# Third quarter of w1 ahead of batch 0's last q slot, tile 1's turn ahead of the second quarter's matmuls, new planned load rates, and one masked product for batch 0's kv

## The chip, the cores and the metric

The kernel runs on one core of a Trainium2 chip. The metric is the device time of the whole program in microseconds (us). Engines are named as in the profile: PE (matmul), PEld (its weight loads), DVE (VectorE), ACT (ScalarE), POOL (GpSimd), SP (SyncE).

## The reference

```python
def _attn_ref(q, k, v, g_norm):                     # 8 batches, 8 heads, 576 rows, 64 wide
    kv = np.einsum('bhsd,bhse->bhde', k, v)
    out = np.einsum('bhsd,bhde->bhse', q, kv)
    rms = np.sqrt(np.mean(out * out, axis=-1, keepdims=True) + 1e-06)
    return out / rms * g_norm

def _moe_ref(x, g_ln, w_ch1, w_ch2):                # x: the above as (8, 576, 512)
    xn = (x - mu) / np.sqrt(var + 1e-06) * g_ln
    return x + np.maximum(xn @ w_ch1, 0.0) @ w_ch2  # 512 -> 2048 -> 512
```

## The kernel before

The kernel does not fix the order of its instructions by hand. Each piece of work is added as a step with an engine, a planned duration, a key (lower goes first) and its inputs; a small planner then plays the program through, with planned rates for the loads, and the start times of that play give each engine its order. Once built, the order is fixed: an engine waits for the next instruction in its order even if a later one is ready (in the changed kernel PE stood 0.66 us for one load while the next one in its order had landed, see below). A planned rate moves no byte, but can change the order.

The rows are handled in 36 tiles of 128. A tile of attention output is normed (DVE and ACT), turned, that is transposed, by PE (`xT` in the profiles), multiplied with the four quarters of w1 (16 matmuls a group in the first two blocks of four tiles) and then with the four quarters of w2. A q slot is the part of a batch's q that one tile needs. The loads of the first 44 us run through one queue from POOL (the comments on the right and the lines with dots are added, for what is left out):

```python
    pool_load(("k", 0, 0), load_kv(kb, k, 0, 0, 4), rate6)
    # ... k, v and q of batch 0, in pieces
    pool_load(("q", 0, 1), load_slot(qp[0], q, 0, 1), rate1)
    load_w(0, 1)                                              # first quarter of w1
    pool_load(("q", 0, 2), load_slot(qp[0], q, 0, 2), rate1)
    load_w(1, 1)
    pool_load(("q", 0, 3), load_slot(qp[0], q, 0, 3), rate1)  # last q slot: tile 3 needs it
    load_w(2, 1)
    load_w(3, 1)
    # ... later: w2's first quarter, k and v of batch 1, w2's second quarter, q of batch 1,
    #     the other quarters of w2
```

The product kv of two heads is a 128x128 block of which only the two 64x64 blocks on the diagonal are wanted. Before, ACT zeroed the target once, and then DVE and ACT each copied one of the blocks out of PSUM, one after the other:

```python
        for u in (0, 1):
            eng, cost = (("DVE", dve_cost), ("ACT", act_cost))[u]
            ab.append(add(eng, *cost(64 * (h1 - h0) // 2), -59 + i, [s, z0],
                          lambda h0=h0, h1=h1, u=u: kv_out(
                              0, h0 // 2, h1 // 2, (nc.vector, nc.scalar)[u], u == 1)))
```

In the planner, PE may hold still for a step that is ready up to `NEAR` = 0.35 us later, if its key is below -3:

```python
                    near = [d for d in cand if d[0] <= t + NEAR and d[1] < c[1] - 0.7
                            and c[0] + c[2].occ > d[0] + 0.1 and (e != "PE" or d[1] < -3)]
```

Of the kernel before, what the change touches and what calls it, by code (L numbers as in the profile page):

```python
# [14 lines left out]
def kernel(  # L15
# [11 lines left out]
    nc = tc.nc  # L27
    f32 = mybir.dt.float32
# [68 lines left out]
    def add(eng, occ, dur, key, deps, fn, dma=None, alloc=None, main=False, lag=0.0):  # L97
        s = Step()
        s.eng, s.occ, s.dur, s.key, s.fn = eng, occ, dur, key, fn
        s.deps = [d for d in deps if d is not None]  # L100
        s.dma, s.alloc, s.main, s.frees, s.behind = dma, alloc, main, None, None
        s.start = s.done = None
        s.lag = lag
        steps.append(s)
        return s
# [83 lines left out]
    def dve_cost(n, rate=0.96, fix=0.075):  # L189
        return n / 1000 / rate + fix, n / 1000 / rate + fix + 0.085  # L190
# [14 lines left out]
    nc.vector.memset(eps_attn, EPS_ATTN)  # L205
    eps_ln = consts.tile([128, 1], f32, name="eps_ln")
    nc.vector.memset(eps_ln, EPS_LN)
    warm = consts.tile([128, 1], f32, name="warm")
    nc.scalar.activation(warm, eps_ln, func=AF.Sqrt)

# [49 lines left out]
    def load_slot(dst, src, b, t, h0=0, h1=H):  # L260
        def fn():
            nc.gpsimd.dma_start(  # L262
                dst[:, t, h0:h1, :],
                src[b, h0:h1, 0:512, :].rearrange("h (p t) d -> p t h d", t=4)[:, t, :, :])
        return fn, 128 * (h1 - h0) * 256
# [65 lines left out]
    def pool_load(name, fnb, rate=425.0, deps=()):  # L331
        fn, nb = fnb
        s = add_dma("POOL", 0, deps, fn, nb, rate)
        load.setdefault(name, []).append(s)
# [4 lines left out]
    def load_w(c, which):  # L339
        dst, src = ((w1, w1_src), (w2, w2_src))[which - 1]  # L340
        def fn():
            if which == 1:
                nc.gpsimd.dma_start(dst[c], src[:, :, c * 512:(c + 1) * 512])  # L343
            else:
                nc.gpsimd.dma_start(dst[c], src[:, c * 4:(c + 1) * 4, :])
        pool_load(("w", which, c), (fn, 512 * 512 * 4))

    def identity_fn():
        make_identity(nc, identity)
# [1 line left out]
    def load_w_kv1():  # L351
# [17 lines left out]
    load_w(0, 1)  # L369
    pool_load(("q", 0, 2), load_slot(qp[0], q, 0, 2), rate1)  # L370
    load_w(1, 1)
    pool_load(("q", 0, 3), load_slot(qp[0], q, 0, 3), rate1)
    load_w(2, 1)
    load_w(3, 1)


    z0 = add("ACT", 0.5, 0.6, -90, [],
             lambda: nc.scalar.memzero(kv_pack[0].rearrange("p a b -> p (a b)")))
    z1 = [pool_do(0.5, f) for f in (
        lambda: nc.gpsimd.memset(qp[0][no_fifth(0), 4, :, :], 0.0),  # L380
        lambda: nc.gpsimd.memset(qp[1][no_fifth(1), 4, :, :], 0.0),
# [78 lines left out]
    def kv_out(b, h0, h1, eng, upper):  # L460
        dst, src = kv_pack[b % 3], att[b]["kv", h0]
        p = slice(D, 128) if upper else slice(0, D)
        f = slice(D, 128) if upper else slice(0, D)
        if eng is nc.scalar:
            eng.copy(dst[p, h0:h1, f], src[p, h0:h1, f])
        else:
            eng.tensor_copy(dst[p, h0:h1, f], src[p, h0:h1, f])  # L467

    def t_out(n, h0=0, h1=H):
        bs, t = TILES[n]  # L470
# [190 lines left out]
    for h0, h1 in PARTS:  # L661
        add_q_turn_pe(0, 0, load["q", 0, 0, h0], -57 + h0 / 4, ("DVE", "ACT")[h0 // 4], h0, h1)
    for t in (1, 2, 3):
        q_turned = add_q_turn_pe(0, t, load["q", 0, t], (-4.5, pos[1] - 3.7, pos[3] - 9)[t - 1],
                                 ("ACT", "ACT", "DVE")[t - 1])
        if t == 2:
            behind_first = q_turned
# [3 lines left out]
    for i, (h0, h1) in enumerate(((0, 4), (4, 6), (6, 8))):  # L671
        hps = range(h0 // 2, h1 // 2)
        w = (h1 - h0) / 8
        s = add("PE", 1.36 * w, 1.36 * w + 0.25, -60 + i, load["v", 0, h0] + [k0p[h0 // 4]],
                lambda hps=hps, i=i: kv_mm(0, hps), alloc="kvt")
        ab = [s]
        for u in (0, 1):
            eng, cost = (("DVE", dve_cost), ("ACT", act_cost))[u]
            ab.append(add(eng, *cost(64 * (h1 - h0) // 2), -59 + i, [s, z0],
                          lambda h0=h0, h1=h1, u=u: kv_out(  # L680
                              0, h0 // 2, h1 // 2, (nc.vector, nc.scalar)[u], u == 1)))
        s.frees = ab[-1]
        kvs.append(ab[1:])
        if i == 0:
            kv_first = s
        else:
            urgent.append(s)
        kv_mm_done = s
# [104 lines left out]
    def plan_tile(n):  # L793
        bs, t = TILES[n]
        m, i = divmod(n, 4)
        p = pos[n]
        dn = done[n]
        deps = []
        for b in bs:
            deps += adone[b]["kv"] + adone[b]["qT", t]  # L800
        if n >= 12:
            deps.append(main_at(okey[n] - EARLY))
        def cost(c, h0, h1):
            return c((h1 - h0) * D)
        halves = PARTS if n in HALVED else ((0, H),)

        q0 = okey[n] if n // 4 not in FINE else p - 12
        xs = []
        for h0, h1 in halves:
            hh = dict(h0=h0, h1=h1)  # L810
            w = (h1 - h0) / H
            q0 = p - 12 if n // 4 in FINE else okey[n]
            d = kvs[len(xs)] + [adone[0]["qT", 0][len(xs)]] if n in HALVED else deps
            o = add("PE", 0.23 * len(bs) * w, 0.23 * len(bs) * w + 0.2, okey[n], d,
                    lambda hh=hh: t_out(n, **hh), alloc="out")
            if n in HALVED:
                urgent.append(o)
            sq = add("ACT", *cost(act_cost, h0, h1), q0 + 4,
                     [o] + [done[n - 3]["red"] if n >= 3 else None], lambda hh=hh: t_sq(n, **hh))
            red = add("DVE", 0.6 * w, 0.6 * w + 0.08, q0 + 5, [sq], lambda hh=hh: t_red(n, **hh))  # L820
            o.frees = xg = add("DVE", *cost(dve_cost, h0, h1), q0 + 5.5, [sq, gn_done],
                               lambda hh=hh: t_xg(n, **hh))
            rms = add("ACT", 0.2, 0.3, q0 + 5.8, [red], lambda hh=hh: t_rms(n, **hh))
            inv = add("DVE", 0.12, 0.2, q0 + 6.5, [rms], lambda hh=hh: t_inv(n, **hh))
            xdeps = [inv, xg]
            if n >= XB:
                xdeps.append(done[n - XB]["store"])
            extra = 0.08 if n < N_SUM else 0
            occ, dur = cost(dve_cost, h0, h1)
            xs.append(add("DVE", occ + extra, dur + extra, q0 + 7, xdeps, lambda hh=hh: t_x(n, **hh)))  # L830
        for b in bs:
            adone[b].setdefault("outs", []).append(o)
        dn["red"] = red
        few = n < N_SUM
        mean = add("DVE", 0.15 if few else 0.8, 0.2 if few else 0.9, q0 + 7.5, xs, lambda: t_mean(n))
        m1_before = blk[m - 3]["m1done"] if m >= 3 else None
        turned = []
        for h0, h1 in ((0, 4), (4, 8)) if n in HALF_TURN else halves:
            ff = dict(f0=h0 * D, f1=h1 * D)
            w = (h1 - h0) / H  # L840
            xc = add("DVE", 0.6 * w + 0.06, 0.6 * w + 0.15, q0 + 8, [mean, load["gl"][0]],
                     lambda ff=ff: t_xc(n, **ff))
            if n < N_PE_TURN:
                tp = add("PE", 0.23 * w, 0.23 * w + 0.22, q0 + 8.2, [xc, ident, m1_before],
                         lambda ff=ff: t_turn_pe(n, **ff), alloc="kvt")
                if n in HALVED:
                    urgent.append(tp)
                tp.frees = add("ACT", *cost(act_cost, h0, h1), q0 + 8.5, [tp],
                               lambda ff=ff: t_turn_out(n, **ff))
                turned.append(tp.frees)  # L850
            else:
                turned.append(add_dma("SP", q0 + 9, [xc, m1_before], lambda: t_turn_dma(n),
                              0.5e3, 1.0, occ=1.235, lat=0.25, tail=0.42))
        dn["xT"] = turned
        if n in HALVED:
            behind_first.deps.append(tp)
        var = [mean]
        if few:
            var.append(add("ACT", 0.68, 0.83, p + 5, xs + dn["xT"], lambda: t_s2(n)))
        blk[m].setdefault("var", []).extend(var)  # L860
        if m in FINE or i == 3:
            vd = var if m in FINE else blk[m]["var"]
            e = last_pos[n if m in FINE else 4 * m] - 6
            if few:
                vd = [add("DVE", 0.33, 0.4, e, vd, lambda: b_var(n))]
            s = add("ACT", 0.2, 0.3, e + 1, vd, lambda: b_std(n))
            r = add("DVE", 0.12, 0.2, e + 2, [s], lambda: b_rstd(n))
            for j in ((n,) if m in FINE else range(4 * m, 4 * m + 4)):
                done[j]["rstd"] = r
# [139 lines left out]
```

## Time and profile before

| what | before |
|---|---|
| time, median of 3 runs | 294.01 us (293.96 to 294.26) |
| PE busy | 283.5 us, 97% of a span of 292.3 |
| ACT, DVE, POOL busy | 49%, 56%, 22% |
| second quarter of w1 lands (PE waits for it) | 19.09 us |
| q of batch 1 lands (ACT permutes it, PE turns it) | 38.82 us |

PE is the bound, so the question is where PE stands still. The first line of part 4 of the page, "by engine", sums up the chain of work that ended last:

```profile
PE 85%; DMA 10%; POOL 3%; issue 0%; ACT 0%; DVE 0%; POOLq 0%
```

The 10% of DMA are the two loads of the table. For exact sums I use **holes**: the start of a matmul less the start of the one before it and its pitch, 0.0557 us for 128 columns and 0.2158 for 512, both read from the trace's start times. The profile's own idle figure is some 0.16 us smaller for the same hole, since the end of a matmul is modelled. In the kernel before, the holes from 17 us on are 1.42 (w1's second quarter), 0.29 and 0.23 (behind tile 1's turn) and 0.55 (turn of batch 1's q). There are none above 0.06 after that.

### The profile page before, as it was taken

How to read it: one execution, taken by the hardware profiler on the slowest of the kernel's cores; microseconds unless marked ns; L12 is line 12 of the kernel's file. 1: busy time of each engine (PE TensorE's matmuls, PEld its weight loads, DVE VectorE, ACT ScalarE, POOL GpSimd, SP SyncE). 2: the span in 40 equal slices, each digit the busy share in tenths (PEclk: the TensorE clock that was granted, in tenths of full speed). 3: DMA queues.
4: the chain of work that ended last, by engine and by line, in shares of the span. 5: the costliest groups of instructions: out<-in, count | busy, mean ns of one | idle time of the engine just before them, and what ended most of it. 6: DMA issues, size and time to landing. Idle time of an engine off the chain costs nothing.

```text
span 292.3 us, 5180 instructions
## 1 busy us (share of the span) xinstructions
PE 283.5 (97%) x2056; PEld 160.9 (55%) x2056; DVE 164.3 (56%) x358; ACT 143.2 (49%) x292; POOL 65.7 (22%) x93
## 2 busy tenths in 40 slices
PE   8769999999999999999999999999999999999995
PEld 6659944977745445444544445444544444444444
DVE  1587038569973997557655775477557755320022
ACT  3469953787846612761276127611761177017400
POOL 8983230106407204504060406000000000000000
PEclk9999999999999999999999999999999999999999
DMA  7999999944999998996999499912201310220012
GB/s 97 184 199 205 204 198 171 251 85 66 177 201 112 162 138 206 117 167 161 134 119 219 60 184 116 195 54 91 56 18 54 92 54 18 57 87 21 0 74 72
DMA packets 108716, 35.60 MB, mean 122 GB/s; under 512 B 87187, under 2 KB 104467, under 8 KB 108692
## 3 DMA queue, kind: packets, MB, share of 16 engines
q0 software_dynamic: 72624, 18.35, 66.6%
q1 hardware_dynamic: 35828, 16.79, 25.9%
q8 instruction: 16, 0.26, 0.4%
q10 hardware_dynamic: 240, 0.13, 0.2%
q14 instruction: 8, 0.07, 0.1%
HBM read 36.70 MB, written 9.44 MB: 158 GB/s over the span
## 4 chain that ended last, share of the span: by engine, by line
PE 85%; DMA 10%; POOL 3%; issue 0%; ACT 0%; DVE 0%; POOLq 0%
PE mm_ps L640 41%; PE mm_ps L621 33%; DMA qb<-in_q_dram 7%; PE mm_ps L606 5%; DMA w<-in_moe_w_ch_dram 3%; PE out_ps L475 3%; PE kv_ps L452 2%; POOL qp L262 1%; POOL vb L241 1%; PE xT_ps L556 1%; POOL kb L241 1%; PE qT_ps L411 0%; POOL w L343 0%; ACT qp L391 0%; POOL identity masks.py:197 0%
## 5 line engine op out<-in xcount | busy, mean ns | idle before, releaser
L640 PE MATMUL mm_ps<-w,m 128*128 128x512 bf16 (+2 forms) x608 | 129.8, 368 | 0.0
L621 PE MATMUL mm_ps<-xT,w 128*128 128x512 bf16 x448 | 100.6, 379 | 0.0
L628 ACT ACTIVATE m<-mm_ps 128x512 bf16<-128x512 f32 x112 | 66.8, 597 | 51.2 <-PE mm_ps L621 50.3
L640 PEld LDWEIGHTS <-m 128*128 128x128 bf16 x608 | 57.1, 98 | 60.3
L621 PEld LDWEIGHTS <-w 128*128 128x128 bf16 x448 | 43.1, 98 | 48.8
L497 DVE TENSOR_REDUCE ss<-sq 128x8 f32<-128x512 f32 (+1 forms) x37 | 24.6, 668 | 47.7 <-ACT sq L488 47.7
L647 DVE SCALAR_TENSOR_TENSOR x<-mm_ps,rstd,x 128x512 f32<-128x512 f32 (+2 forms) x38 | 27.2, 719 | 42.1 <-PE mm_ps L640 42.1
L488 ACT ACTIVATE sq<-out_ps 128x512 f32<-128x512 f32 (+1 forms) x37 | 21.5, 583 | 38.9 <-PE out_ps L475 38.9
L606 PE MATMUL mm_ps<-xT,w 128*128 128x128 bf16 x512 | 30.9, 219 | 1.6 <-DMA w<-in_moe_w_ch_dram 1.3
L606 PEld LDWEIGHTS <-w 128*128 128x128 bf16 x512 | 29.3, 98 | 2.8 <-DMA w<-in_moe_w_ch_dram 1.4
L549 DVE SCALAR_TENSOR_TENSOR xc<-x,mv,gl 128x512 bf16<-128x512 f32 (+1 forms) x38 | 27.2, 722 | 1.1
L492 DVE TENSOR_TENSOR xg<-out_ps,gn 128x512 f32<-128x512 f32 (+1 forms) x37 | 24.7, 668 | 0.2
L613 ACT ACTIVATE m<-mm_ps 128x512 bf16<-128x512 f32 x32 | 18.7, 598 | 3.3 <-PE mm_ps L606 2.9
L730 POOL COPY mark<-xT 128x1 bf16<-128x1 bf16 x15 | 7.0, 464 | 58.0 <-DMA xT<-xc 54.0
L501 ACT ACTIVATE rms<-ss,eps_attn 128x8 f32<-128x8 f32 (+1 forms) x37 | 11.0, 298 | 12.4 <-DVE ss L497 12.2
L527 DVE TENSOR_TENSOR x<-xg,inv 128x512 f32<-128x512 f32 x24 | 16.6, 691 | 0.8
L543 DVE BATCH_NORM_STATS2 stats<-x 128x6 f32<-128x512 f32 x24 | 16.6, 690 | 0.5
L475 PEld LDWEIGHTS <-qT 128*128 128x128 bf16 x160 | 11.4, 98 | 7.2 <-ACT qT L391 1.1
L475 PE MATMUL out_ps<-kv_pack,qT 128*128 128x128 bf16 x160 | 14.5, 219 | 0.7 <-ACT qT L391 0.7
L467 DVE CAST kv_pack<-kv_ps 64x256 bf16<-64x256 f32 (+2 forms) x17 | 6.6, 390 | 9.8 <-PE kv_ps L452 5.9
L452 PEld LDWEIGHTS <-kp 128*128 128x128 bf16 (+1 forms) x168 | 10.3, 99 | 2.5 <-DVE kp L393 0.4
L269 POOL DMA_DIRECT2D qp<-in_q_dram x5 | 11.4, 2282 | 0.7 <-issue 0.7
(63 smaller groups left out, 176.9 us busy)
## 6 DMA issues: line engine op xcount, KB each, us to landing
out_dram<-x SPq DMA_DIRECT2D x30, 256.0 KB, 2.9
w<-in_moe_w_ch_dram POOLq DMA_DIRECT2D x8, 512.0 KB, 12.2
vb<-in_v_dram POOLq DMA_DIRECT2D x6, 512.0 KB, 11.9
kp<-in_k_dram POOLq DMA_DIRECT2D x5, 512.0 KB, 9.3
qp<-in_q_dram POOLq DMA_DIRECT2D x5, 512.0 KB, 10.8
out_dram<-x SPq DMA_DIRECT2D x10, 128.0 KB, 3.4
qb<-in_q_dram POOLq DMA_DIRECT2D x2, 512.0 KB, 18.2
qp<-in_q_dram POOLq DMA_DIRECT2D x10, 64.0 KB, 9.3
```

What stands on the lines that cost most here:

```text
L475: nc.tensor.matmul(o3[:, hp, :], lhsT=att[b]["qT"][:, 4 * t + hp, :], rhs=kv_pack[b % 3][:, hp, :], start=(i == 0), stop=(i == len(bs) - 1))
L488: nc.scalar.activation(sq[:, h0:h1, :], st[n]["ps", h0][:, h0:h1, :], func=AF.Square)
L492: nc.vector.tensor_mul(xg[:, h0:h1, :], st[n]["ps", h0][:, h0:h1, :], gn.to_broadcast([128, h1 - h0, D]))
L497: nc.vector.tensor_reduce(ss[:, h0:h1, :], st[n]["sq"][:, h0:h1, :], axis=AX.X, op=ALU.add)
L527: nc.vector.tensor_mul(x, st[n]["xg"], inv)
L549: nc.vector.scalar_tensor_tensor(xc[:, f0:f1], in0=st[n]["x"][:, f0:f1], scalar=blk[m]["mv"][:, i, 0:1], in1=gl[:, f0:f1], op0=ALU.subtrac ...
L606: nc.tensor.matmul(ps[:, d, :], lhsT=w1[c][:, kk, d * 128:(d + 1) * 128], rhs=blk[m]["xT"][:, kk, i * 128:(i + 1) * 128], start=(kk == 0), ...
L613: nc.scalar.activation(st[n]["m1"][:, c, :, :], st[n]["m1ps", c], func=AF.Relu)
L621: nc.tensor.matmul(ps, lhsT=w1[c][:, kk, d * 128:(d + 1) * 128], rhs=blk[m]["xT"][:, kk, :], start=(kk == 0), stop=(kk == nKm - 1))
L628: nc.scalar.activation(blk[m]["m1", c][:, d, :], blk[m]["m1ps", g], func=AF.Relu)
L640: nc.tensor.matmul(st[n]["m2ps", f0], lhsT=m1_piece(n, c, d), rhs=w2[c][:, d, f0:f1], start=(c == 0 and d == 0), stop=(c == 3 and d == 3))
L647: nc.vector.scalar_tensor_tensor(x[:, f0:f1], in0=st[n]["m2ps", f0], scalar=blk[m]["rstd"][:, i, :], in1=x[:, f0:f1], op0=ALU.mult, op1=AL ...
```

## The change

Its intent: have w1's third quarter in time for a PE that gets ahead; fill PE's wait for w1's second quarter with the turn of tile 1; shorten the path from kv to tile 0 by taking the copies off ACT. The planned rates of the first two quarters are set closer to what the loads take.

```diff
+    diag = consts.tile([128, 1, 128], f32, name="diag")
+    nc.vector.memset(diag, 0.0)
+    for p in (slice(0, D), slice(D, 128)):
+        nc.vector.memset(diag[p, :, p], 1.0)
@@ planned rate of a weight load
-        pool_load(("w", which, c), (fn, 512 * 512 * 4))
+        pool_load(("w", which, c), (fn, 512 * 512 * 4), 355.0 if which == 1 and c < 2 else 425.0)
@@ order of loads
+    load_w(2, 1)
     pool_load(("q", 0, 3), load_slot(qp[0], q, 0, 3), rate1)
-    load_w(2, 1)
     load_w(3, 1)
-    z0 = add("ACT", 0.5, 0.6, -90, [],
-             lambda: nc.scalar.memzero(kv_pack[0].rearrange("p a b -> p (a b)")))
@@ kv of batch 0: the pair of copies (above) gives way to
+        nc.vector.tensor_mul(kv_pack[b % 3][:, h0:h1, :], att[b]["kv", h0][:, h0:h1, :],
+                             diag.to_broadcast([128, h1 - h0, 128]))
@@ key of the turn of q slots 1 to 3
-(-4.5, pos[1] - 3.7, pos[3] - 9)[t - 1]
+(-4.5, pos[1] - 3.7, -3.2)[t - 1]
@@ key of tile 0's first half x
-q0 + 7
+q0 + (4.8 if h1 < H else 7)
@@ key of a tile's turn
-q0 + 8.2
+-3.5 if n == 1 else q0 + 8.2
```

More of the change, by code (lines that the diff above doesn't have):

```diff
@@ L462, in kv_out, with kv_out_masked @@
         p = slice(D, 128) if upper else slice(0, D)
-        f = slice(D, 128) if upper else slice(0, D)
-        if eng is nc.scalar:
-            eng.copy(dst[p, h0:h1, f], src[p, h0:h1, f])
-        else:
-            eng.tensor_copy(dst[p, h0:h1, f], src[p, h0:h1, f])
+        eng.tensor_copy(dst[p, h0:h1, p], src[p, h0:h1, p])
+    def kv_out_masked(b, h0, h1):
+        nc.vector.tensor_mul(kv_pack[b % 3][:, h0:h1, :], att[b]["kv", h0][:, h0:h1, :],
+                             diag.to_broadcast([128, h1 - h0, 128]))
     def t_out(n, h0=0, h1=H):
@@ L663 @@
     for t in (1, 2, 3):
-        q_turned = add_q_turn_pe(0, t, load["q", 0, t], (-4.5, pos[1] - 3.7, pos[3] - 9)[t - 1],
+        q_turned = add_q_turn_pe(0, t, load["q", 0, t], (-4.5, pos[1] - 3.7, -3.2)[t - 1],
                                  ("ACT", "ACT", "DVE")[t - 1])
@@ L675 @@
                 lambda hps=hps, i=i: kv_mm(0, hps), alloc="kvt")
-        ab = [s]
-        for u in (0, 1):
-            eng, cost = (("DVE", dve_cost), ("ACT", act_cost))[u]
-            ab.append(add(eng, *cost(64 * (h1 - h0) // 2), -59 + i, [s, z0],
-                          lambda h0=h0, h1=h1, u=u: kv_out(
-                              0, h0 // 2, h1 // 2, (nc.vector, nc.scalar)[u], u == 1)))
-        s.frees = ab[-1]
-        kvs.append(ab[1:])
+        s.frees = add("DVE", *dve_cost(64 * (h1 - h0)), -59 + i, [s],
+                      lambda h0=h0, h1=h1: kv_out_masked(0, h0 // 2, h1 // 2))
+        kvs.append([s.frees])
         if i == 0:
@@ L829, in plan_tile @@
             occ, dur = cost(dve_cost, h0, h1)
-            xs.append(add("DVE", occ + extra, dur + extra, q0 + 7, xdeps, lambda hh=hh: t_x(n, **hh)))
+            xs.append(add("DVE", occ + extra, dur + extra, q0 + (4.8 if h1 < H else 7), xdeps, lambda hh=hh: t_x(n, **hh)))
         for b in bs:
@@ L843, in plan_tile @@
             if n < N_PE_TURN:
-                tp = add("PE", 0.23 * w, 0.23 * w + 0.22, q0 + 8.2, [xc, ident, m1_before],
+                tp = add("PE", 0.23 * w, 0.23 * w + 0.22, -3.5 if n == 1 else q0 + 8.2, [xc, ident, m1_before],
                          lambda ff=ff: t_turn_pe(n, **ff), alloc="kvt")
```

## The prediction

> **What bounds the kernel now.** I read the busy times on the page first, then the chain that ended last, then the timeline of PE through the first 24 us, then those of DVE and ACT there, and last the DMA issues one by one in short windows, to get the landing of each load.
>
> ```profile
> PE 283.5 (97%) x2056; PEld 160.9 (55%) x2056; DVE 164.3 (56%) x358; ACT 143.2 (49%) x292; POOL 65.7 (22%) x93
> ...
> PE   8769999999999999999999999999999999999995
> ```
>
> PE is the bound. From its third slice on it has no hole worth a tenth; only the first 20 us (slices one to three) have idle time. PE's useful work is not touched by this change, so the time can only move by as much idle as is taken out of, or put into, PE's row. The chain shows what holds the head up.
>
> ```profile
> 8.73 0.86 POOL qp L262
> 9.59 9.50 DMA w<-in_moe_w_ch_dram
> 19.09 0.28 issue
> 19.37 19.45 DMA qb<-in_q_dram
> 38.82 0.02 issue
> 38.84 0.63 ACT qp L391
> 39.52 0.40 PE qT_ps L411 x4
> ```
>
> Two loads stand in it: the second quarter of w1, landing at 19.09, and all of q of batch 1, landing at 38.82 after 19.45 us in the queue. From 39.52 to 288.83 the chain is PE alone. The PE timeline shows what the first load costs.
>
> ```profile
> 15.56 0.68 PE L556 MATMUL xT_ps<-identity,xc 128*128 128x128 bf16 x4 [0.65 <-DVE xc L549]
> 16.08 0.39 PE L411 MATMUL qT_ps<-identity,qp 128*128 128x128 bf16 x4
> 16.31 1.34 PE L606 MATMUL mm_ps<-xT,w 128*128 128x128 bf16 x16
> 17.48 0.39 PE L475 MATMUL out_ps<-kv_pack,qT 128*128 128x128 bf16 x4
> 19.13 1.07 PE L606 MATMUL mm_ps<-xT,w 128*128 128x128 bf16 x16 [1.26 <-DMA w<-in_moe_w_ch_dram]
> 20.04 0.28 PE L556 MATMUL xT_ps<-identity,xc 128*128 128x128 bf16 x2
> 20.15 0.39 PE L411 MATMUL qT_ps<-identity,qp 128*128 128x128 bf16 x4
> 20.37 0.28 PE L556 MATMUL xT_ps<-identity,xc 128*128 128x128 bf16 x2
> 20.77 1.28 PE L606 MATMUL mm_ps<-xT,w 128*128 128x128 bf16 x16
> 21.89 0.39 PE L475 MATMUL out_ps<-kv_pack,qT 128*128 128x128 bf16 x4
> 22.11 1.95 PE L606 MATMUL mm_ps<-xT,w 128*128 128x128 bf16 x32
> ```
>
> The reader is to see three holes. At 17.87 PE has run out of work and sits 1.26 us for w1's second quarter. At 20.37 the turn of tile 1 begins its last half; two matmuls issue in 0.11, so PE is free at 20.48, but the first group of tile 1 starts at 20.77: 0.29 us, in which ACT copies the turned tile out. Sixteen matmuls at 0.0557 each take 0.89, so that group could end its issue at 21.66; the next begins at 21.89, another 0.23 us, waiting for the second half of the same copy. After that PE is without a hole but for 0.39 us at 39.1, the end of the wait for batch 1's q.
>
> [...] POOL's loads land in issue order (15.2 w1 first quarter, 16.0 q slot 2, 19.1 w1 second, 19.7 q slot 3, 22.2 w1 third, about 24.8 w1 fourth), so swapping two loads moves only those two. [...] the trace has 0.41 for the 128x256 product xg out of PSUM. [...]
>
> **The change part by part.**
>
> Mask. Three pairs of copies out of PSUM go (ACT 0.26, 0.21, 0.21; DVE 0.28, 0.22, 0.22, each DVE one behind ACT's), with ACT's memzero of 0.40 at 2.15, when ACT was idle anyway.
>
> ```profile
> 8.98 0.28 DVE L467 CAST kv_pack<-kv_ps 64x128 bf16<-64x128 f32 x1 [2.37 <-ACT kv_pack L465]
> ...
> 11.01 0.22 DVE L467 CAST kv_pack<-kv_ps 64x64 bf16<-64x64 f32 x1 [0.82 <-ACT kv_pack L465]
> 11.84 0.22 DVE L467 CAST kv_pack<-kv_ps 64x64 bf16<-64x64 f32 x1 [0.61 <-ACT kv_pack L465]
> 11.98 0.40 DVE L497 TENSOR_REDUCE ss<-sq 128x4 f32<-128x256 f32 x1
> ```
>
> The first pair took 8.69 to 9.26, 0.57 us; one product of 128x256 should take 0.41. The two others took 0.46 each[...]. More important, DVE's reduction at 11.98 stood behind the third cast, though its square had ended at 11.38, and that square stood behind a cast on ACT. From 11.98 to 20.2 DVE is busy without a break worth naming, so what DVE gains here its whole chain gains: I take 0.4 us. The second half's q lands at 11.45 either way, so the gain is not the full 0.6. Tile 0's xc, which ended at 15.46 and 15.90, then ends near 15.05 and 15.5; tile 1's, 18.6 and 19.04 before, ends near 18.15 and 18.6. This alone gives nothing at the end, for PE meets w1's second quarter at 19.1 just the same.
>
> Turn of tile 1 in front. With tile 1's xc ready by 18.6, its four transposes (4 x 0.055 = 0.22) move into the hole of 1.26, and ACT's copies (0.71 for the pair) lie beside the wait, so the 0.29 and 0.23 behind the turn vanish. Sum: 0.74 us. The first group of tile 1 needs only w1's first quarter; if its copy is out by about 18.9 and the plan puts it ahead, up to 0.3 more is filled. I count 0.1.
>
> Loads. Slot 3 is 256 KB, about 0.65 us of queue (19.1 to 19.7). Without it in front, w1's third quarter lands near 21.6 rather than 22.2. PE after 19.1 has three groups in hand, 3 x 0.89 = 2.7, up to 21.8; the third quarter is then just in time. In the old order it would have come 0.4 late, which would eat half the gain. Slot 3's q lands near 22.2 instead of 19.7, and tile 3's path moves with it: its output product ran at 21.89 and its turn at 27.69; from product to finished xc are 5.4 us. New: product near 23.1, xc near 28.2, turned and copied by 29; tile 3's first group is due at 27.91 + 3 x 0.89 = 30.6, less the gain of 0.8, at 29.8. It fits, with under 1 us to spare. The transfer rates in the plan (355 for two quarters) move no byte; they make its order expect w1's second quarter later, close to where the trace has it.
>
> Down the line. Bytes queued ahead of batch 1's q are the same, so it lands at 38.8 still and its turn can't run before 39.5. If PE's order there were kept, PE would come 0.8 earlier and wait 1.2, and all the gain would be lost. The plan's correction (two times 1.05 MB/355 less 1.05 MB/425, 0.97 us) pushes the planned landing later by about as much as PE gains, so I expect one more group of w2 (0.86) ahead of the turn and a wait near the present 0.4. I take 0.1 off for it.
>
> Sum: 0.22 + 0.52 + 0.1 - 0.1 = 0.74, so 294.01 - 0.74 = 293.27, say 293.3.
>
> **The rivals.** One: the gain is given back at batch 1's q. For it: the chain goes through that load, and the queue is full from 3.4 to about 44 us. Against it: sixteen groups of w2 are ready beside it, and the plan can put one ahead. It would make 294.0, or 294.3 with rounding. Two: slot 3 becomes the wait; ACT is 9.43 us busy of the 10 from 20 to 30, so tile 3's copies may slip past 29.8. A slip of one ACT activation is 0.6 us; time 293.9. Three: it goes better. If tile 1's first group is wholly ahead of w1's second quarter (0.89 in the hole) and the wait at 39.1 goes as well (0.39), the gain is 0.22 + 0.52 + 0.89 + 0.39 = 2.0 and the time 292.0. Against it: the xc of 18.6 leaves no time for 0.89 before 19.1. Four: the new memsets delay POOL's first issue[...].
>
> **Range and chances.** All of these lie within 2 us of 294, and two per cent is 5.9 us; the whole of PE's removable idle after 16 us is 1.26 + 0.52 + 0.39 = 2.2 us. So faster by 2% is next to impossible, and slower by it would need the static order to break somewhere. The range is 292.5 (rival three in half) to 294.1 (rival one in full).
>
> **What would show it.** Right: DVE's first reduction near 11.4; the turn of tile 1 ahead of the groups that wait for w1's second quarter, with that wait cut below 1.1 us; no hole behind the turn; w1's third quarter landing near 21.6; a wait below 0.6 at batch 1's q; all PE work after 45 us shifted by 0.7 as one. Wrong: a wait of 1 us or more before the turn of batch 1's q, one before tile 3's first group, a later first load, or holes after 45 us from a changed order of the plan.

Passages that no trace of this case shows are cut from the prediction where marked. No term of its sum is among them: 0.22 + 0.52 + 0.1 - 0.1 = 0.74. The mask's 0.4, which is not in the sum, is the estimate from the 0.6 between the end of the square at 11.38 and the start of the reduction at 11.98. In the trace of before, the DMA moved between 176 and 205 GB/s in each stretch from 3.4 to 44 us (the "full" queue), and the groups behind the hole of 1.26 ran at 0.0557 us a matmul.

## The result

| | before | changed |
|---|---|---|
| median | 293.99 us (4 runs, 293.86 to 294.26) | 293.67 us (4 runs, 293.43 to 293.84) |
| ratio | | 0.9987, 95% interval 0.997 to 1.0005 |
| second set (with e8) | 294.27 (11 runs, 293.77 to 294.76) | 294.27 (5 runs, 294.03 to 294.86), ratio 1.0007, 0.9994 to 1.002 |

Ratios are the mean time of one kernel's runs over that of the other's of the same rounds, so not quite the ratio of the medians. The second set was taken among the experiments (run e8). Taken together: **no difference clear of noise**. Two traces whose heads are alike (PE's clock was released at 7.96 before and 8.03 after, and the last piece of batch 0's v landed at 11.01 and 11.00) show what the change does inside, so I read those. By released I mean that the record lists full speed from there: in both traces idle matmuls of 128 columns start 0.107 apart ahead of it and 0.056 behind it. The page's busy line, its PE row and the summary of the chain, after:

```profile
PE 283.9 (97%) x2057; PEld 161.1 (55%) x2057; DVE 165.2 (57%) x361; ACT 142.6 (49%) x288; POOL 65.6 (22%) x93
...
PE   8879999999999999999999999999999999999995
...
PE 91%; DMA 4%; POOL 3%; issue 0%; DVE 0%; POOLq 0%
```

The slices look alike, but the chain has changed: neither of the two loads of before is in it. The chain in order of time, after:

```profile
9.62 1.44 POOL w L348 x2
11.06 11.47 DMA qp<-in_q_dram
22.53 0.05 issue
22.57 0.40 PE qT_ps L414 x4
```

It now goes through q slot 3, the load that was moved back; it lands at 22.53. From there it is PE alone. PE's timeline over the head (start, length, instructions, in brackets the idle time before and what ended it), after:

```profile
16.14 1.34 PE L609 MATMUL mm_ps<-xT,w 128*128 128x128 bf16 x16
17.31 0.39 PE L478 MATMUL out_ps<-kv_pack,qT 128*128 128x128 bf16 x4
18.53 0.68 PE L559 MATMUL xT_ps<-identity,xc 128*128 128x128 bf16 x4 [0.84 <-DVE xc L552]
19.22 2.85 PE L609 MATMUL mm_ps<-xT,w 128*128 128x128 bf16 x48
22.57 0.40 PE L414 MATMUL qT_ps<-identity,qp 128*128 128x128 bf16 x4 [0.50 <-DMA qp<-in_q_dram]
22.81 1.06 PE L609 MATMUL mm_ps<-xT,w 128*128 128x128 bf16 x16
...
36.48 3.62 PE L643 MATMUL mm_ps<-w,m 128*128 128x512 bf16 x16
39.93 0.61 PE L414 MATMUL qT_ps<-identity,qp 128*128 128x128 bf16 x8
```

The reader is to see three things. Tile 1's turn (18.53) does stand in the old hole, and three groups then run without a break from 19.22. Then PE stands for slot 3's turn, 0.50 by the profile, a hole of 0.66 by starts; w1's third quarter, the second of the two loads whose issue begins at 9.62, had landed at 21.69, and its group waited behind the turn. And at 36.48 there are four groups of w2 (16 matmuls of 512 columns) after one before kv, so five in all ahead of the turn of batch 1's q, which then runs without a wait.

A ledger from the starts in the two traces:

| PE reaches | before | changed | ahead by |
|---|---|---|---|
| tile 0's first group of w1 | 16.31 | 16.14 | 0.17 |
| w2's first group | 34.17 | 34.27 | -0.10 |
| tile 4's first group | 51.23 | 50.77 | 0.46 |
| first group of the third block | 83.80 | 83.52 | 0.28 |
| start of the last matmul | 288.60 | 288.32 | 0.28 |

So the head, where the change works, ends 0.10 behind. An earlier start brought 0.17 and smaller holes around tile 1's turn 0.50 (1.94 became 1.00, 0.27 and 0.17), and slot 3 took 0.66 of these 0.67; a hole of 0.06 at w1's fourth quarter, which landed at 25.06, and smaller ones took the rest. The 0.17 and the 0.50 can't be credited to mask and turn apart: the last of the three holes ends when w1's second quarter lands (19.17, and 19.09 before), and a still earlier start would only have made it longer. The gain of 0.28 arose at 39 us: the hole of 0.55 at the turn of batch 1's q is gone. A new hole of 0.17 at 60.6, before an output product, took part of it back. From the third block on both run the same 204.80 us.

On DVE, the mask, after:

```profile
8.67 0.42 DVE L469 TENSOR_TENSOR kv_pack<-kv_ps,diag 128x256 bf16<-128x256 f32 x1 [2.06 <-PE kv_ps L455]
...
11.59 0.29 DVE L469 TENSOR_TENSOR kv_pack<-kv_ps,diag 128x128 bf16<-128x128 f32 x1 [0.50 <-PE kv_ps L455]
11.80 0.41 DVE L500 TENSOR_REDUCE ss<-sq 128x4 f32<-128x256 f32 x1
```

The products take 0.42 and 0.29; 0.41 was predicted for the first. But the last stands ahead of the reduction and waits for PE's last kv, and that for the last piece of v; so the reduction starts at 11.80, only 0.18 earlier.

### The profile page after: what moved, and what is told of

It reads as the page before. It is cut to its first block, busy times and chain, and to the rows that moved or that the text cites. A ratio compares the mean times of both kernels' runs of the same rounds, so it can differ in the third digit from the quotient of the medians.

```text
span 292.0 us, 5183 instructions
## 1 busy us (share of the span) xinstructions
PE 283.9 (97%) x2057; PEld 161.1 (55%) x2057; DVE 165.2 (57%) x361; ACT 142.6 (49%) x288; POOL 65.6 (22%) x93
## 4 chain that ended last, share of the span: by engine, by line
PE 91%; DMA 4%; POOL 3%; issue 0%; DVE 0%; POOLq 0%
PE mm_ps L643 43%; PE mm_ps L624 33%; PE mm_ps L609 9%; DMA qp<-in_q_dram 4%; PE out_ps L478 3%; PE kv_ps L455 3%; POOL qp L267 1%; PE xT_ps L559 1%; POOL w L348 1%; POOL vb L246 1%; POOL kb L246 1%; PE qT_ps L414 0%; POOL identity masks.py:197 0%; DVE x L650 0%; POOL identity masks.py:199 0%
## 5 line engine op out<-in xcount | busy, mean ns | idle before, releaser
L500 DVE TENSOR_REDUCE ss<-sq 128x8 f32<-128x512 f32 (+1 forms) x37 | 24.8, 669 | 48.4 <-ACT sq L491 48.4
L466 DVE CAST kv_pack<-kv_ps 64x256 bf16<-64x256 f32 x14 | 5.9, 422 | 12.9 <-PE kv_ps L455 12.8
```

The source lines that it names most:

```text
L500: nc.vector.tensor_reduce(ss[:, h0:h1, :], st[n]["sq"][:, h0:h1, :], axis=AX.X, op=ALU.add)
```

## The experiments

Theory A was formed from the ledger: the head's gain was lost at slot 3's turn, and what is left comes from the order at the turn of batch 1's q. Every result was correct. Times are medians, with the ratio to the kernel before of the same rounds.

### e1: the planned rates alone

```diff
 (kernel before)
-        pool_load(("w", which, c), (fn, 512 * 512 * 4))
+        pool_load(("w", which, c), (fn, 512 * 512 * 4), 355.0 if which == 1 and c < 2 else 425.0)
```

> The kernel before with nothing but the change's new planned rates for the first two quarters of w1. No byte moves differently; on PE the only change of order that matters is that one group of w2's second quarter stands ahead of the turn of batch 1's q (five groups of w2 before it, not four). Theory A (the 0.3 us of the change come from the wait for batch 1's q, which this order hides, and the head gives nothing): the wait of 0.39 at 39.1 is gone, the head up to 24.1 is as before, and the time is 0.25 to 0.4 below before, the same as the whole change. Rival B (the head's loads and turn give the gain): time within 0.1 of before.

Measured: 293.66 against 293.80, ratio 0.9995 (0.9983 to 1.0007). In the trace the last matmul starts at 288.36, 0.24 earlier than before and within 0.04 of the whole change. The trace fits theory A on that; the timed gain of 0.14 is less than the 0.25 to 0.4 that it forecast, and within the noise. Theory A was wrong on the way: the new rates also put half of tile 1's turn ahead of the second quarter's group, so the head did gain, and w2's first group came at 33.82, 0.35 before that of the kernel before. PE's timeline at the q turn of e1:

```profile
36.02 3.62 PE L640 MATMUL mm_ps<-w,m 128*128 128x512 bf16 x16
39.53 0.92 PE L411 MATMUL qT_ps<-identity,qp 128*128 128x128 bf16 x8
40.28 1.03 PE L640 MATMUL mm_ps<-w,m 128*128 128x512 bf16 x4
```

Eight turns take 0.92 rather than 0.61, as the second four wait for ACT's permutes, which run from 38.85 to 41.03. With holes of 0.29 there and 0.20 behind it, 0.49 of a lead was given back. What follows: a change of the plan that moves no byte gives all that the traces show for the whole change; and a head that is 0.45 earlier than the changed kernel's (33.82 against 34.27) ends at the same time, because batch 1's q lands when it lands (ACT permutes it from 38.85, and from 38.71 in the changed kernel).

### e2: the mask undone

The changed kernel with the memzero and the three pairs of copies as in the kernel before, without the diagonal.

```diff
-        s.frees = add("DVE", *dve_cost(64 * (h1 - h0)), -59 + i, [s], ... kv_out_masked ...)
+        for u in (0, 1): ... kv_out on DVE, then on ACT, as in the kernel before ...
```

> The changed kernel with the three pairs of copies out of PSUM and the memzero in place of the masked product and the diagonal; PE's order is the changed kernel's but for one idle matmul. Theory A: tile 0 and tile 1 come about 0.17 later, and that is taken up by waits for loads (w1's second quarter at 19.1, q slot 3 at 22.5), so PE at 24.15 and the time are the changed kernel's within 0.1. Rival B: the mask's 0.17 stays, time 0.17 above the changed kernel.

Measured: 293.81 against 293.80, ratio 1.0003 (0.9991 to 1.0015). In this trace the last piece of batch 0's v landed at 11.53 rather than 11.00, and with the copies in place of the mask the head is 0.69 later than the changed kernel's at tile 0's first group (16.83 against 16.14). PE's timeline of e2:

```profile
16.83 1.34 PE L606 MATMUL mm_ps<-xT,w 128*128 128x128 bf16 x16
...
22.43 0.39 PE L411 MATMUL qT_ps<-identity,qp 128*128 128x128 bf16 x4
...
34.04 1.03 PE L640 MATMUL mm_ps<-w,m 128*128 128x512 bf16 x4
```

That makes it a sharper test than meant: the turn of slot 3 ran at 22.43 without a wait, w2's first group came at 34.04, 0.23 *before* the changed kernel's, and the last matmul at 288.34 against 288.32. A head that is later by 0.69 lost nothing. In the traces the mask's 0.17 can't be seen in the end, which speaks against rival B. The times can't decide: 293.81 lies 0.14 above the 293.67 of the changed kernel, near rival B's 0.17, but the two were not timed in the same rounds, and 0.14 is within the noise.

### e3: slot 3's turn planned later

```diff
-lag=2.0 if t == 4 else 0.0
+lag=2.0 if t == 4 else 0.6 if t == 3 else 0.0
```

> The changed kernel with q slot 3's turn planned 0.6 us later, so that a group of w1's third quarter stands ahead of it on PE. Theory A: the wait of 0.50 us (0.68 with the matmuls' modelled end taken off) for slot 3 at 22.1 is gone and PE reaches w2's first group near 33.6 instead of 34.27; but kv of batch 1 now stands ahead of w2's first group and its inputs are ready only near 35.1, and the turn of batch 1's q stands after four groups of w2 again, so PE waits about 1.4 us at kv and some tenths at the q turn: all is lost again, time 293.9 to 294.8. Rival C (the wait for slot 3 was the only loss): time near 293.0.

Measured: 295.03 against 293.80, ratio 1.0047 (1.0027 to 1.0066), slower, clear of noise. The wait for slot 3 is gone as expected, but the loss came elsewhere than I had said. PE's timeline of e3:

```profile
24.33 5.52 PE L609 MATMUL mm_ps<-xT,w 128*128 128x128 bf16 x96
29.69 0.39 PE L559 MATMUL xT_ps<-identity,xc 128*128 128x128 bf16 x4
30.75 3.73 PE L609 MATMUL mm_ps<-xT,w 128*128 128x128 bf16 x64 [0.67 <-ACT xT L566]
```

The turn of tile 3 now stands directly ahead of tile 3's first group, and PE waits 0.67 (a hole of 0.84) for ACT to copy it out. In the changed kernel two groups stand between the two. At kv there was no wait; at the q turn 0.21 and 0.28. The time near 293.0 of rival C did not come. But the edit moved more than slot 3's turn: tile 3's input was done at 28.53 in this trace, 1.16 before its turn on PE at 29.69, so it was the new order and not slot 3's landing that made this wait. An order with slot 3's turn late and tile 3's turn early was not tried, and rival C is not settled. The trace also does not carry the whole loss: its last matmul starts 0.31 later than before, and it is the fastest of six runs between 294.41 and 296.63.

### e4: the later waits planned later too

```diff
 (e3, and:)
+                    qperm.lag = 1.5
-        s.lag = 5.0 if b > 2 else 2.0 if b == 2 else 0.0
+        s.lag = 5.0 if b > 2 else 2.0 if b == 2 else 3.0
```

> As the run with slot 3's turn planned later, and with kv of batch 1 planned 3.0 us and the permutes of its q 1.5 us behind their loads' planned landing: two groups of w2 ahead of kv, six ahead of the q turn. Theory A (any gain in the head counts only if PE has other work ahead of every later wait for a load): no wait above 0.3 us on PE after 20 us, PE at 50 us about 0.6 us ahead of the changed kernel, time 292.8 to 293.2. Rival D (tile 3, later loads or ACT then stop PE): holes between 24 and 50 us, time 293.5 or more.

Measured: 295.24 against 293.80, ratio 1.0041 (1.0028 to 1.0054), slower. There is no hole at kv or at the q turn, which stands after six groups of w2, but the 0.84 at tile 3 stays, and a larger hole comes at 61. PE's timeline of e4:

```profile
60.18 0.22 PE L478 MATMUL out_ps<-kv_pack,qT 128*128 128x128 bf16 x1
61.45 0.56 PE L478 MATMUL out_ps<-kv_pack,qT 128*128 128x128 bf16 x7 [1.05 <-DMA qT<-qp]
```

The products of the tile that two batches share wait for a transpose by DMA, a hole of 1.21. The transpose is no later than in the changed kernel, measured from tile 4's first group (61.41 less 51.50, and 60.75 less 50.77). What differs is PE's order: the kv product of the next batch, 1.12 of work, stands ahead of these products there (59.45) and behind them here (61.85). The edit had moved more than meant. Rival D was right: the 0.84 lies where it said, the 1.21 further on.

### e5: slot 3 loaded first again

```diff
 (changed kernel)
-    load_w(2, 1)
     pool_load(("q", 0, 3), load_slot(qp[0], q, 0, 3), rate1)
+    load_w(2, 1)
```

> The changed kernel with q slot 3 loaded ahead of w1's third quarter again, as before. On PE slot 3's turn then stands ahead of tile 1's first group; from w2's first group on the order is the changed kernel's. Theory E (moving the load ahead made slot 3 late and cost the head's whole gain): slot 3 lands by 19.9, its turn costs no wait, w1's third quarter (landing 22.2 to 22.5) meets PE with a hole of at most 0.25, so the sum of PE's holes from 19 to 34 us falls from about 1.0 to 0.5 or less and PE reaches w2's first group 0.4 to 0.6 earlier; 0.2 to 0.5 of that is lost again at the turn of batch 1's q, which still stands after five groups of w2. Time 0.0 to 0.4 below the changed kernel. Rival F (the load order was right, w1's third quarter is what PE would wait for): a hole of 0.5 or more at 22 us before a group of w1's third quarter, time as the changed kernel or above.

Measured: 294.35 (293.61 to 294.63) against 294.27, ratio 1.0000 (0.9986 to 1.0015); the changed kernel (e8) 294.27. The profiled run was the fastest of the five and not typical: its last matmul starts at 287.84. What it shows of the waits is clear, though. The chain in order of time of e5:

```profile
12.38 12.32 DMA w<-in_moe_w_ch_dram
24.71 0.04 issue
24.75 2.85 PE mm_ps L609 x48
```

Slot 3 costs no wait, and w1's third quarter none either (its group starts at 22.21 behind an output product, without a hole); but then PE stands for w1's fourth quarter, which lands at 24.70, a hole of 0.52. Theory E is right on slot 3 and on w1's third quarter (the holes from 19 to 34 sum to 0.52, and w2's first group came at 33.92, 0.35 earlier, where 0.4 to 0.6 was expected), rival F's hole at 22 is absent, and yet the time did not fall: a PE that was not held at slot 3 (0.66 in the first trace of the changed kernel) was held at w1's fourth quarter (0.52). The loads land one after the other, in the order of their issue: in the trace of before at 15.2, 16.0, 19.1, 19.7, 22.2 and about 24.8 (w1's first quarter to its fourth, with q slots 2 and 3 between).

### e6: the same, with the later waits planned later

```diff
 (e5, and:)
+                    qperm.lag = 1.0
-        s.lag = 5.0 if b > 2 else 2.0 if b == 2 else 0.0
+        s.lag = 5.0 if b > 2 else 2.0 if b == 2 else 2.0
```

> As the run with the loads put back, and with kv of batch 1 planned 2.0 us and the permutes of its q 1.0 us behind their loads' planned landing: two groups of w2 ahead of kv, six ahead of the q turn. Theory E with A (what is won in the head counts only where PE has other work ahead of the later waits): no hole above 0.3 on PE from 20 to 56 us; time 0.4 to 0.9 below before, and 0.1 to 0.5 below the run with the loads put back. Rival D (the later q turn stops PE further on, as in the run that held all): a new hole above 0.5 after 50 us, and the time at or above before.

Measured: 294.23 against 294.27, ratio 1.0012 (0.9993 to 1.003). No hole at the q turn or after it, but again 0.52 at w1's fourth quarter and 0.21 at its third. No gain: the expectation missed. The lead that was to be held had been spent at 25 us.

### e7: the kernel before with planned rates and tile 1's turn first

```diff
 (e1, and:)
-                tp = add("PE", 0.23 * w, 0.23 * w + 0.22, q0 + 8.2, [xc, ident, m1_before],
+                tp = add("PE", 0.23 * w, 0.23 * w + 0.22, -3.5 if n == 1 else q0 + 8.2, [xc, ident, m1_before],
```

> The kernel before with the new planned rates and tile 1's turn first, but with the old loads' order and the pairs of copies instead of the mask. PE's order is that of the run with the loads put back. Theory E: the holes at the turn of tile 1 fall from 1.94 (1.42 + 0.29 + 0.23) to about 1.5, no wait for slot 3, time 0.3 to 0.6 below before, within 0.2 of the run with the loads put back. Rival G (the mask is needed for the turn to be in time for w1's second quarter): the turn comes 0.17 later than in the changed kernel and the time is 0.2 or more above the run with the loads put back.

Measured: 294.10 against 294.27, ratio 0.9995 (0.9983 to 1.0008), inconclusive as a time. In this trace the clock was released only at 12.98, the last piece of batch 0's v landed at 11.47, and tile 0's first group started at 17.47, 1.16 later than before. After tile 1's turn PE has no hole above 0.09 to the end, and the last matmul starts at 288.66, 0.06 later than before. A head that is more than 1 us late costs almost nothing, since the waits that it would have met are gone. The holes at tile 1's turn were 1.27 (1.00 and 0.27), less than the 1.5 expected. On rival G this trace can't speak; e7's median lies 0.25 below that of e5, where rival G expected 0.2 or more above, but that is within the noise.

### e8: the changed kernel again

No edit; the changed kernel on the chip of e5 to e7.

> The changed kernel as it is, on the same chip as the three others, to compare them directly. Time 0.2 to 0.4 below before; the wait before slot 3's turn between 0.3 and 0.7 again[...].

Measured: 294.27 (294.03 to 294.86) against 294.27, ratio 1.0007 (0.9994 to 1.002). The gain of 0.3 did not come again. The last piece of batch 0's v landed at 11.45, 0.45 later than in the first trace, tile 0's first group started at 16.58, the wait for slot 3 was a hole of 0.20 only, w2's first group came at 34.09, and then the chain ran through batch 1's q again. The chain in order of time of e8:

```profile
19.26 19.90 DMA qb<-in_q_dram
39.16 0.02 issue
39.18 1.15 ACT qp L394 x2
```

It landed at 39.16 rather than 38.69 as in the first trace of the same kernel (where ACT's permute starts at 38.71), and PE had holes of 0.10, 0.29 and 0.20 there. The last matmul starts at 288.58: the gain of 0.28 in the first trace hangs on a load that lands 0.5 us earlier in one run than in another.

### e9 to e12: an attempt to take the clock's jitter out

The release of PE's clock lay between 7.6 and 13.0 us in the ten traces. I suspected the two broadcasts of the scales, matmuls with one row, which hold PE for 2.4 us from 2.39, of delaying it, and moved them behind the first kv product (what the traces say of this suspicion stands at the end of this part); the planner then fills their place with full idle matmuls. The same edit went into the kernel before (e9), the changed kernel (e10), the one with the loads put back (e11), and that one with q of batch 1 loaded ahead of w2's second quarter (e12).

```diff
+    spreads = {}
-        s = add("PE", *((1.8, 2.0) if dst == "gl" else (0.4, 0.6)), -98, ...
+        s = spreads[dst] = add("PE", *((1.0, 1.2) if dst == "gl" else (0.3, 0.5)), -98, ...
             kv_first = s
+            for x in spreads.values():
+                x.deps.append(s)
 (e12 only:)
+        pool_load(("q", 1), load_q(1, 0, 4), rate4, [])
         load_w(1, 2)
-        pool_load(("q", 1), load_q(1, 0, 4), rate4, [])
```

> The kernel before, with the two broadcasts of the scales (one-row matmuls, 2.4 us on PE from 2.39) moved behind the first kv product, their place taken by full idle matmuls. In the ten traces so far the clock of PE was released between 7.6 and 13.0 us, and the full-speed stretch lasts a whole number of 3.413 us. Theory H [...]: now the release comes between 4.4 and 7.9, the times of the runs lie within 0.3 of each other (the kernel before ranged over 1.0), and the median falls 0.1 to 0.4 below before. Rival I (the spread comes from the loads' landing): release as before or spread as before.

> The changed kernel with the same move of the broadcasts, so that the change can be read without the clock's jitter. Theory A: 0.2 to 0.4 below the steady kernel before, all of it from the turn of batch 1's q standing one group later; the wait for slot 3 at 22 is 0.6 to 0.9, as the head is early in every run. Rival J (the 0.3 of the first comparison was chance): within 0.1 of the steady kernel before.

> The steady changed kernel with slot 3 loaded ahead of w1's third quarter again. Theory E: no wait for slot 3; 0.2 to 0.4 of hole at w1's fourth quarter near 24.5 takes its place and 0.2 to 0.4 comes back at the q turn; 0.1 to 0.4 below the steady changed kernel. Rival F: equal to it or above.

> As the steady kernel with the loads put back, and batch 1's q loaded ahead of w2's second quarter, so that it lands near 36.2 and w2's second quarter near 38.9. Theory K (the landing of batch 1's q caps what the head can give): no wait above 0.3 at the q turn, and 0.2 to 0.6 below the run without the swap; w2's second quarter is first used after four groups of w2, kv and the turns, near 39, so it may cost up to 0.2. Rival L (the queue, not one load, sets the pace): the wait moves to w2's second quarter with 0.4 or more, and the time is as without the swap.

Measured, with 293.99 (11 runs) for the kernel before: e9 294.12, ratio 1.0007 (0.9995 to 1.0019); e10 293.79, 1.0002 (0.9977 to 1.0027), its six runs lying between 293.37 and 293.90 but for one of 296.14; e11 294.14, 1.0006 (0.9991 to 1.0022); e12 294.24, 1.0016 (0.9991 to 1.0041). The five runs of e9 lie within 0.44 of each other, where 0.3 was expected (0.81 for eleven of the kernel before); those of e10 to e12 spread over 1.5 to 2.8. None is faster than the kernel before. Half of theory H held: the clock was released earlier, at 5.49, 6.19, 3.78 and 4.46, all but the third inside the 4.4 to 7.9 expected (the author's estimate; its reason, which no trace shows, is cut). The other half failed: it was taken back at 12.32, 9.61, 10.60 and 11.29, for one or two stretches of 3.41 us. PE's timeline of e10:

```profile
8.46 0.33 PE L962 MATMUL idle_ps<-blank 128*128 128x128 bf16 x3
8.72 1.55 PE L322 MATMUL scale_ps<-scales,ones 1*128 1x512 f32 x4
10.20 0.39 PE L415 MATMUL qT_ps<-identity,qp 128*128 128x128 bf16 x2
10.47 0.80 PE L456 MATMUL kv_ps<-vb,kp 96*128 96x128 bf16 x6
```

With the clock taken back, the six kv matmuls take 0.80, against 0.49 in the changed kernel, and ten idle ones at 13.41 take 1.27, against 0.72 in e8. The edit is rejected, and e9 to e12 can't be used as a jitter-free comparison. e10 lies below e9 by 0.33 in the medians, as in the first comparison, but with its slow run e10's interval spans everything. e12 shows one thing free of the clock: with q of batch 1 loaded earlier, ACT permuted it at 36.80, PE had no hole at its turns nor at w2's second quarter, and tile 4's first group came at 51.33, 0.09 ahead of e11's 51.42. Both heads were 1.7 to 1.8 later than the changed kernel's (first group at 17.87 and 17.96), so they met no wait that the earlier landing could have removed; K and L stay open.

The first ten traces already speak against the suspicion. PE's last kv product of batch 0 waits for the last piece of v, before and after:

```profile
11.05 0.51 PE L452 MATMUL kv_ps<-vb,kp 96*128 96x128 bf16 x6 [0.21 <-DMA vb<-in_v_dram]
...
11.05 0.51 PE L455 MATMUL kv_ps<-vb,kp 96*128 96x128 bf16 x6 [0.17 <-DMA vb<-in_v_dram]
```

| trace | clock released | last piece of v lands | tile 0's first group | from landing to group |
|---|---|---|---|---|
| before, e1, e2 (copies) | 7.96, 8.30, 9.81 | 11.01, 10.97, 11.53 | 16.31, 16.27, 16.83 | 5.30, 5.30, 5.30 |
| changed, e3, e4, e6, e8 (mask) | 8.03, 8.77, 8.98, 8.85, 10.60 | 11.00, 10.84, 11.58, 11.13, 11.45 | 16.14, 15.96, 16.71, 16.26, 16.58 | 5.14, 5.13, 5.13, 5.13, 5.13 |
| e5 (mask) | 7.63 | 10.98 | 16.28 | 5.30 |
| e7 (copies) | 12.98 | 11.47 | 17.47 | 6.00 |

In eight of the ten the head follows the landing to 0.01, wherever the clock was released; the mask is worth 0.16 to 0.17 there. In e5 PE waited 0.16 more for the turn of q slot 2, which landed at 16.00. Only in e7, where the release came after the landing, is there a further 0.70. So in these ten traces, up to a release at 10.60, it is a load and not the clock that moves the head.

## Why the prediction was right or wrong

The measured 293.67 lies in the range of 292.5 to 294.1, and that nothing would move by 2% was nearly certain and came true. The forecast 293.3 was half a gain too far, and two of the steps behind it were wrong; that they had opposite signs, which brought the sum closer, is luck.

**Bound and places: right.** (The row of slices shows idle time up to its third slice, so "from its third slice on" should read fourth.) PE is the bound, its useful work did not change, and every difference between the kernels lies ahead of 83.5 us; behind it all runs looked at without missing records take 204.80 us.

**Mask: right in the first product, wrong in what it brings.** The product of 128x256 took 0.42 against 0.41, the time of a product of that size in the trace of before. Those of 128x128 took 0.29. "I take 0.4 us" is the term that was mis-sized; it measured 0.17, because the last product waits for the last piece of v and stands ahead of the reduction. It was predicted to give nothing at the end; the trace of e2 agrees.

**Turn of tile 1 in front: right.** 0.74 was predicted from the transposes in the hole and the two waits behind the turn. Just before slot 3's turn PE was 0.65 ahead: the 60th matmul after tile 0's first of w1 starts at 21.24, before at 21.89. Nearly all that is missing is the load: w1's second quarter landed at 19.17 rather than 19.09. "No hole behind the turn" did not hold: 0.27 stayed inside it, as tile 1's second half was ready only at 18.87, and 0.17 behind it. The further 0.1, for a part of tile 1's first group, did not come: PE holds only the transposes between 18.53 and 19.22.

**Loads: the step that failed.** w1's third quarter landed near 21.7 as predicted (21.6). For slot 3 the prediction followed only tile 3's path ("It fits, with under 1 us to spare") and did not ask what stands behind slot 3's turn in PE's own order. The new key of -3.2 lets the plan hold PE for that turn, planned to come 0.35 late at most; the load came at 22.53 rather than 22.2, and PE stood for 0.66 with w1's third quarter already there. That ate the head's gain in full: w2's first group came at 34.27 against 34.17. In e3 the group went first and this wait was gone, but that order made tile 3 wait; whether another order keeps the gain was not tried. A sum is wrong, too: 23.1 and 5.4 make 28.5 for tile 3's xc, not 28.2. It did not matter; the product ran at 23.70 and xc was done at 28.12.

**Down the line: wrong in sign.** "I take 0.1 off" was to be a small loss at batch 1's q. Its order was foreseen rightly (one more group of w2 ahead of the turn), but as the head brought no lead, the extra group hid the old hole of 0.55, and this is where the 0.28 of the trace came from. e1 shows that the planned rates alone, which move no byte, reach the same end.

**Rivals.** One (the gain is given back at batch 1's q) is what e1 and e8 show, with 0.49 and 0.59 of holes there and behind it. Two (slot 3 becomes the wait) came true for the changed kernel, at the turn rather than at ACT's copies; ACT's copy was the wait in e3. Three fell. Four fell: POOL's first issue stands at 1.30 as before, with the three memsets in place.

**What the prediction lacked** is the run-to-run movement of the same size as the effect: the kernel before itself ranged from 293.52 to 294.76 over the four sets of runs. Tile 0's first group started between 15.96 and 17.47 in the first ten traces, with the landing of batch 0's v and, in e7, a late release of the clock, though e2 and e7 show that a later head costs almost nothing; and batch 1's q landed (by ACT's first permute) between 38.39 and 39.32. That the second of these explains the times' spread was not tested, as each timed run has no trace.

## What to carry to other kernels

In this kernel one queue of loads feeds the head, and an engine that ran ahead met the next load (0.66 at slot 3; 0.52 at w1's fourth quarter in e5). So follow a moved load to the first instruction that waits for it in the fixed order of the bounding engine, and ask what stands ready behind that instruction. A gain in the head counted only up to the last load that everything passes (e1's head was 0.45 earlier than the changed kernel's, 33.82 against 34.27, and its last matmul started at 288.36 against 288.32), so look first at what other work can stand ahead of that load's first user; in the traces here a planned rate did as much as the whole change. And when the expected gain is about the spread of the runs, compare traces that are alike at their start, do not trust a difference of medians from one set of runs, and look for the landing that a late head waits for before blaming the clock.

## What the traces show of the clock and the queue

- In e9 and e10 the clock was taken back with PE never idle for more than 0.9 us between matmuls by the profile: released at 5.49 and 6.19, taken back at 12.32 and 9.61 for 3.41 and 6.83 us. In e10 the stretch of 3.41 us just before holds one-row fp32 matmuls and a wait of 0.87; whether the one-row matmuls or the waits did it was not separated.
- The full-speed stretch was 283.31 us, 83 times 3.413, in nine of the first ten traces (82 times in e7); the stretch for which the clock was taken back in e9 took 3.41. The release, with the first matmul at 1.00 and one-row matmuls from 2.39 to 4.78, came between 7.6 and 13.0. With these moved (e9 to e12) it came between 3.78 and 6.19, in e11 only 2.78 after the first matmul.
- POOL's loads landed in the order of their issue in every trace, as far as landings show it. A landing behind the queue moved between runs of one kernel: for the changed kernel batch 1's q landed at 38.7 in one trace and at 39.2 in another.
